# Recurrence output computed transposed, by 32-column matmuls on quarters of the array

## The chip, the cores and the metric

The kernel runs on one core of one Trainium2 chip. The metric is the device time of one launch in microseconds, as the median of several runs. A profile is one execution recorded by the hardware: its span is the time from its first to its last recorded instruction, and its own time holds a little more around it. The engines are TensorE (PE; its weight loads PEld), VectorE (DVE), ScalarE (ACT), GpSimd (POOL) and SyncE (SP), whose queue issues the DMAs.

## What is computed

A gated linear recurrence over 768 steps for 4 batches of 8 heads of 48 channels, and then a feed-forward layer over the 3072 tokens (d_model 384, d_ff 2048). Inputs and output are fp32.

```
def _attn_ref(q, k, v, alpha):
    for t in range(S):
        state = alpha[:, :, t, :, None] * state + np.einsum('bhd,bhe->bhde', k[:, :, t], v[:, :, t])
        y[:, :, t] = np.einsum('bhd,bhde->bhe', q[:, :, t], state)

def _moe_ref(x, w_in, w_out):
    r = np.maximum(x @ w_in, 0.0)
    return (r * r) @ w_out
```

Here x is y with the heads of a token side by side: 8 heads of 48 make the 384 columns. The matmuls of the kernel are in bf16 with fp32 sums.

## The kernel before

**Tiling.** The 3072 tokens are 24 chunks of 128, six for each batch. Within a chunk the recurrence is written as matmuls. L is the log of alpha; a matmul with a triangle of ones (`e_p0`) sums it along the chunk; A and Ainv are its exponentials; qA = q·A and kI = k·Ainv. qA and kI are transposed on TensorE, for two heads at a time (four pairs of heads, `NP`; a head takes 48 of 64 rows), and copied to SBUF as qkT. The scores sc = kI·qA (`e_p2`, by halves of the array, one head in each) are masked into sm. The state of 48x48 a head goes through the PSUM tile st: `e_ps` adds kI·v, VectorE scales it (`e_stm`), ScalarE casts it to sb (`e_sb`).

**The output of a chunk before.** Its output y lies with tokens on partitions: `e_p3a` (L576) multiplies qkT by the last chunk's sb, four matmuls of 96 columns (left out in the first chunk of a batch), and `e_p3b` (L582) multiplies the masked scores by vb, eight matmuls of 48 columns, both with 128x128 weights and into one PSUM bank, py. The feed-forward part needs x transposed, with the 384 channels on partitions. So `add_tail` (L380) follows: ScalarE casts py to bf16 (xn, L374 with `cast`), TensorE transposes xn in three 128x128 blocks into another bank (`e_p4`, recorded at L257), and VectorE, or ScalarE in the first six chunks, copies these to their 128 columns of xT_big (`e_xT`).

**Three ways to work chunks.** The first four chunks are worked as two supers of two chunks each (`add_super`, L597), where a row holds two neighbouring tokens and 64 rows are one chunk; their score part has 64-row weights. Chunks 4 to 7 are worked singly (`add_chunk`, L401). From chunk 8 on (`PAIRS`) the scores of two chunks are taken in one block (`add_scores`, L508), and `add_back` (L545) follows for each.

**The feed-forward part.** The chunks are grouped 4, 1, 1, 2, 2, and so on (`GN`). For each group, `add_moe1` multiplies w_in by xT_big (16 slices of d_ff, three matmuls each), ScalarE takes the relu, VectorE squares into gT; `add_moe2` multiplies gT by w_out in four quarters for each chunk; ScalarE or VectorE copies the sums out and SP issues the store. The weights arrive in fp32 by DMA, in pieces, and are cast by GpSimd or ScalarE (`load_w`).

**Order.** A planner (`Plan`) writes the order of every engine at build time. Each step is an `Op` with an engine (or several, with a duration for each, of which the one that ends first is taken), a planned duration, its dependencies and a priority. A PE step is ready at the end of what it depends on, plus a slack if that is on another engine: `PE_SLACK` of 0.05 us, and 0.25 us once TensorE's plan is past `PE_CALM` (L36, 25 us). `LEAD` (L330, 3.5) says how many chunks the recurrence may run ahead of the feed-forward part. At run time every engine works its list strictly in that order. The planned durations only make the order.

**PSUM.** Two banks hold sc and st for good; the five others are dealt out by the planner: `GLA_BANKS`, two of them, serve the recurrence of single and double chunks (sums, transposes, second scores, py, px), `SUP_BANKS`, four, that of the supers, and three the feed-forward part. A bank is free again when the step named in `gives` is done. While the planner still sees gaps ahead of the first `add_moe2`, it fills them with matmuls on a zero tile (warm).

Of the kernel before, what the change touches and what calls it, by code (L numbers as in the profile page):

```python
# [8 lines left out]
FP32 = mybir.dt.float32  # L9
# [23 lines left out]

LAT = {"PE": 0.13, "ACT": 0.14, "DVE": 0.13, "POOL": 0.25}
PE_SLACK = 0.05
PE_CALM = 25.0  # L36
PAUSES = [(13.0, 1.0), (18.0, 1.0)]


# [107 lines left out]
def kernel(  # L147
# [97 lines left out]
    nc.gpsimd.memset(kI_s[:, :, :, D:], 0.0)  # L245
    ae_s = big.tile([P, NBUF, 2, NP], FP32)
    nc.vector.memset(ae_s, 0.0)
    xT_big = big.tile([P, KT, n_tok], BF16)

    def pin(ins):  # L250
# [2 lines left out]
    def mm(*a, **kw):  # L253
        pin(nc.tensor.matmul(*a, **kw))  # L254

    def tr(*a):
        pin(nc.tensor.transpose(*a))  # L257
# [11 lines left out]
    def psum(op, shape, dt):  # L269
        i = op.slot.bank  # L270
        return banks[i].tile(shape, dt, name=f"bank{i}")
# [6 lines left out]
    def add(eng, dur, emit, *deps, **kw):  # L278
        return plan.add(Op(eng, dur, emit, deps, **kw))
# [47 lines left out]
    SRC = dict(srcs)  # L327
    EARLY = 2 * 3
    PAIRS = 8
    LEAD = 3.5  # L330

    NS = 2
    SIDE = 0
# [38 lines left out]
    def cast(op, out_t, in_t):  # L372
        if op.eng == "ACT":
            pin(nc.scalar.copy(out_t, in_t))  # L374
        elif op.eng == "DVE":
            pin(nc.vector.tensor_copy(out_t, in_t))  # L376
        else:
            pin(nc.gpsimd.tensor_copy(out_t, in_t))

    def add_tail(s, done, first, g):  # L380
        d = C[s]

        def e_xn():
            d["xn"] = work.tile([P, HD], BF16, name="xn")
            cast(xn, d["xn"], d["py"][:, 0:HD])
        xn = add("ACT", 0.36, e_xn, done, **g)
        first.gives = xn

        def e_p4():
            d["px"] = psum(p4, [P, KT, P], BF16)  # L390
            for j in range(KT):
                tr(d["px"][:, j, :], d["xn"][:, j * P:(j + 1) * P], ident_bf)
        p4 = plan.add(Op("PE", 0.165, e_p4, [xn], takes=GLA_BANKS, lat=0.14, **g))

        def e_xT():
            cast(xT, xT_big[:, :, s * P:(s + 1) * P], d["px"])
        xT = add({"ACT": 0.36, "DVE": 0.27} if s < EARLY else "DVE", 0.27, e_xT, p4, prio=-9.0)
        d["x"] = d["end"] = xT
        p4.gives = xT

    def add_chunk(s):  # L401
        d = C[s]
# [11 lines left out]
        def e_vb():  # L414
            d["vb"] = work.tile([P, H, D], BF16, name="vb", bufs=4)
            pin(nc.gpsimd.tensor_copy(d["vb"], d["vt"]))  # L416
        vb = d["use_vt"] = add("POOL", 0.55, e_vb, d["ld_vt"], old, prio=-5.0)

        def e_p0():
            pm = d["pm"] = psum(p0, [P, 512], FP32)  # L420
# [75 lines left out]
            cp = cpk = add("DVE", 0.61, lambda: e_cp(0, 2 * NP), p1k, **g)  # L496
        p1q.gives = cpk

        d.update(cps=[cp, cpk], mk=mk, vb_op=vb, ae1=ae1, kI=kI, ae=ae)
        if s < PAIRS:  # L500
            add_scores(s, 1)
            add_back(s)
        elif s % 2:
            add_scores(s - 1, 2)
            add_back(s - 1)
            add_back(s)

    def add_scores(s, n):  # L508
        pr = C[s:s + n]
# [32 lines left out]
        for hh, h in enumerate(hold):  # L542
            h.gives = pr[1]["sms"][hh]

    def add_back(s):  # L545
        d = C[s]
        b, c = divmod(s, NCH)
        g = dict(prio=-10.0 + s * 0.01)
        last = c == NCH - 1
        kI, ae, mk, vb, ae1 = d["kI"], d["ae"], d["mk"], d["vb_op"], d["ae1"]  # L550
        cp, (sm0, sm1) = d["cps"][0], d["sms"]

        if not last:
            def e_ps():
                if c == 0:
                    state["ps"] = ps_st.tile([P, NP, 2 * D], FP32, name="st")
                st = d["st"] = state["ps"]
                for p in range(NP):
                    mm(st[:, p, :], lhsT=kI[:, 2 * p:2 * p + 2, :], rhs=d["vb"][:, 2 * p:2 * p + 2, :],
                       start=(c == 0 and p == 0), stop=True, skip_group_check=True)  # L560
            prev = C[s - 1].get("sb") if s else None
            if c == 0 and s:
                prev = C[s - 2]["sb"]
            ps = plan.add(Op("PE", 0.17, e_ps, [mk, vb, ae1, prev], lat=0.16, **g))

            def e_stm():
                st4 = d["st"].rearrange("p n (j e) -> p n j e", j=2)
                pin(nc.vector.tensor_mul(st4, st4, bcast(ae, D)))  # L568
            stm = add("DVE", 0.47, e_stm, ps, ae1, prio=-2.0)

            def e_sb():
                d["sbt"] = work.tile([P, NP, 2 * D], BF16, name="sb")
                pin(nc.scalar.copy(d["sbt"], d["st"]))  # L573
            d["sb"] = add("ACT", 0.37, e_sb, stm, prio=-2.0)

        def e_p3a():  # L576
            d["py"] = psum(p3a, [P, 512], FP32)
            for p in range(NP):
                mm(d["py"][:, 2 * p * D:2 * (p + 1) * D], lhsT=d["qkT"][:, p, :], rhs=C[s - 1]["sbt"][:, p, :],
                   start=(p == 0), stop=False, skip_group_check=True)  # L580

        def e_p3b():  # L582
            if c == 0:
                d["py"] = psum(p3b, [P, 512], FP32)
            for hh in range(2):
                for p in range(NP):
                    h = 2 * p + hh
                    mm(d["py"][:, h * D:(h + 1) * D], lhsT=d["sm"][:, hh, p, :], rhs=d["vb"][:, h, :],
                       start=(c == 0 and hh == 0 and p == 0), stop=True, skip_group_check=True)
        p3a = None  # L590
        if c > 0:
            p3a = plan.add(Op("PE", 0.17, e_p3a, [cp, C[s - 1]["sb"], after(sm0)], takes=GLA_BANKS, **g))
        p3b = plan.add(Op("PE", 0.21, e_p3b, [after(sm1, 0.02), sm0, vb, after(p3a)], takes=None if c else GLA_BANKS, lat=0.15, **g))

        add_tail(s, p3b, p3a or p3b, g)

    def add_super(u):  # L597

# [20 lines left out]
            pin(nc.gpsimd.tensor_copy(d["vb"][t], d["vt"][:, :, t, :]))  # L619
        vb = [add("POOL", 0.55, lambda t=t: e_vb(t), d["ld_vt"], *old, prio=-5.0) for t in any_]  # L620
        d["use_vt"] = vb[1]

        d["pm"] = [None, None]
        HC = HD // 2
# [125 lines left out]
        for ab in any_:  # L750
            s = 2 * u + ab
            c = pair[ab]
            r = slice(HF * ab, HF * ab + HF)
            before = C[s - 1].get("sb") if s else None
            if s < NCH - 1:
                def e_ps(c=c, r=r, s=s):
                    if s == 0:
                        state["ps"] = ps_st.tile([P, NP, 2 * D], FP32, name="st")
                    st = c["st"] = state["ps"]
                    for t in any_:  # L760
                        for p in range(NP):
# [12 lines left out]
                c["sb"] = add("ACT", 0.37, e_sb, stm, prio=-12.0)  # L774

            def e_p3a(c=c, r=r, s=s, ab=ab):
                c["py"] = psum(c["p3a"], [P, 512], FP32)
                for p in range(NP):
                    mm(c["py"][:, 2 * p * D:2 * (p + 1) * D], lhsT=qT(p)[:, ab].rearrange("k t c -> k (t c)"), rhs=C[s - 1]["sbt"][:, p, :],
                       start=(p == 0), stop=False, skip_group_check=True)  # L780

            def e_p3b(c=c, r=r, s=s):
                if s == 0:
                    c["py"] = psum(c["p3b"], [P, 512], FP32)
                for x in any_:
                    for hh in range(2):
                        for p in range(NP):
                            h = 2 * p + hh
                            mm(c["py"][:, h * D:(h + 1) * D], lhsT=d["sm"][p // NH][r, hh, x, p % NH, :], rhs=d["vb"][x][r, h, :],
                               start=(s == 0 and x == 0 and hh == 0 and p == 0), stop=(x == 1), skip_group_check=True)  # L790
            p3a = None
            if s:
                p3a = c["p3a"] = plan.add(Op("PE", 0.2, e_p3a, [cq, before], takes=SUP_BANKS, **g))
            p3b = c["p3b"] = plan.add(Op("PE", 0.5, e_p3b, [*sm, *vb, after(p3a)], takes=None if s else SUP_BANKS,
                                         lat=0.15, **g))
            add_tail(s, p3b, p3a or p3b, g)

    GN = [4, 1, 1, 2, 2, 2, 2, 2, 2, 2, 2, 2]
    assert sum(GN) == NT
# [223 lines left out]
```

## Time and profile before

| | |
|---|---|
| runs of the kernel before, us | 186.7, 185.51, 186.2 (median 186.2) |
| profiled execution, its own time | 185.78 us |
| its span | 184.1 us |
| mean granted TensorE clock | 1.00 |
| TensorE matmuls | 1992 |
| DMA bytes, mean rate | 30.23 MB, 164 GB/s |

The largest groups of TensorE are the two feed-forward matmuls, 73.3 us (xT_big with w_in) and 70.9 us (gT with w_out). A profile row names the source line, engine and operation, then out<-in, the shapes as partitions x elements, a count, and behind the bar the busy time, the mean ns of one, and the idle time of the engine before them with what ended it. A matmul's row gives rows*columns of its weights first and then the shape of what is moved. Matmuls are pipelined: the mean of one is from its start to its modelled end, much longer than the step from one start to the next. All matmuls are recorded at one of two helper lines, L254 (`mm`) and L257 (`tr`), so they are told apart by tiles and shapes. A stretch row gives start:end, its length, busy us with counts in brackets for PE, PEld, DVE, ACT and POOL, the granted clock, the DMA engines' busy share and GB/s. A timeline row gives a start, a length, and what ran, with neighbours of one kind merged.

### The profile page before, as it was taken

The numbers are of one execution on the slowest core, as the hardware profiler recorded it, in microseconds if no ns is written. First come the engines' busy times: TensorE is split into PE (matmuls) and PEld (weight loads), VectorE is DVE, ScalarE is ACT, GpSimd is POOL, SyncE is SP. The second block draws the span as 40 slices with busy tenths as digits, with TensorE's granted clock in tenths as the row PEclk, the third lists the DMA queues.
The fourth block names the chain that finished last, engine by engine and source line by source line (L and its number), as shares of the span: only waits on it lengthen the run. The fifth ranks groups of instructions, "written<-read, shape, count | busy, mean of one in ns | idle before, by whom it ended". The sixth has DMA issues, their size and how long they took to land.

```text
span 184.1 us, 5041 instructions
## 1 busy us (share of the span) xinstructions
PE 178.6 (97%) x1992; PEld 133.4 (72%) x1993; DVE 134.8 (73%) x282; ACT 121.9 (66%) x259; POOL 27.6 (15%) x46
## 2 busy tenths in 40 slices
PE   7899999999999999999999999999999999999993
PEld 3567674666987788767867877777877878767763
DVE  6699669447998888856894997966996988852600
ACT  3565879267998598825939857847848768633721
POOL 6024476612011111111011011010010000000000
PEclk9999999999999999999999999999999999999999
DMA  5999999799898989893989899876701101012012
GB/s 139 276 281 323 318 341 375 156 222 212 168 215 174 220 158 214 180 217 84 205 197 209 202 206 201 192 148 149 187 0 43 46 2 48 0 45 89 0 43 85
DMA packets 101352, 30.23 MB, mean 164 GB/s; under 512 B 93776, under 2 KB 100560, under 8 KB 101328
## 3 DMA queue, kind: packets, MB, share of 16 engines
q1 hardware_dynamic: 101328, 29.91, 69.3%
q8 instruction: 15, 0.25, 0.5%
q14 instruction: 9, 0.07, 0.1%
HBM read 25.17 MB, written 4.72 MB: 162 GB/s over the span
## 4 chain that ended last, share of the span: by engine, by line
PE 90%; DVE 4%; DMA 2%; issue 1%; ACT 1%; DVEq 0%
PE bank L254 77%; PE bank L257 8%; DMA qt<-in_q_dram 2%; PE st L254 2%; PE sc L254 2%; DVE qkT L376 1%; DVE sm L726 1%; DVE sm L534 0%; DVE xT_big L376 0%; ACT r L840 0%; DVE qA_s L663 0%; DVE kI_s L663 0%; DVE qA_s L467 0%; ACT A L647 0%; DVE kI_s L473 0%
## 5 line engine op out<-in xcount | busy, mean ns | idle before, releaser
L254 PE MATMUL bank<-xT_big,w_in_b 128*128 128x256 bf16 (+2 forms) x599 | 73.3, 268 | 0.2
L254 PE MATMUL bank<-w_out_b,gT 128*128 128x384 bf16 (+2 forms) x400 | 70.9, 319 | 0.0
L840 ACT ACTIVATE r<-bank 128x512 bf16<-128x512 f32 x96 | 56.1, 602 | 16.1 <-PE bank L254 14.3
L254 PEld LDWEIGHTS <-w_in_b 128*128 128x128 bf16 x600 | 52.8, 98 | 9.3 <-issue 0.3
L848 DVE TENSOR_TENSOR gT<-r 128x512 bf16<-128x512 bf16 x96 | 42.8, 470 | 10.4 <-ACT r L840 10.1
L254 PEld LDWEIGHTS <-gT 128*128 128x128 bf16 x400 | 36.5, 98 | 18.4
L416 POOL CAST vb<-vt 128x384 bf16<-128x384 f32 x20 | 10.8, 542 | 92.0 <-PE bank L254 49.8
L376 DVE COPY qkT<-bank 128x1024 bf16<-128x1024 bf16 (+1 forms) x26 | 16.5, 646 | 4.8 <-PE bank L257 4.6
L912 ACT COPY ob<-bank 128x384 f32<-128x384 f32 x18 | 8.7, 483 | 16.1 <-PE bank L254 15.8
L534 DVE TENSOR_TENSOR sm<-sc,utri_b 128x512 bf16<-128x512 f32 x24 | 15.4, 683 | 3.0 <-PE sc L254 3.0
L374 ACT CAST xn<-bank 128x384 bf16<-128x384 f32 x24 | 11.2, 486 | 9.2 <-PE bank L254 9.1
L254 PEld LDWEIGHTS <-qkT 64*128 64x128 bf16 (+2 forms) x304 | 10.5, 97 | 5.6 <-issue 2.5
L376 DVE COPY xT_big<-bank 128x384 bf16<-128x384 bf16 x19 | 6.7, 354 | 10.5 <-PE bank L257 10.5
L470 DVE TENSOR_TENSOR qA_s<-qt,Af 128x384 bf16<-128x384 f32 x12 | 10.4, 869 | 2.5 <-ACT Af L439 2.5
L411 ACT ACTIVATE L_s<-at 128x384 bf16<-128x384 f32 x20 | 10.2, 523 | 2.1 <-DMA at<-in_alpha_dram 2.0
L439 ACT ACTIVATE Af<-bank 128x384 f32<-128x384 f32 x12 | 10.4, 865 | 1.6 <-ACT xn L374 1.0
L473 DVE TENSOR_TENSOR kI_s<-kt,Ainv 128x384 bf16<-128x384 f32 x20 | 11.3, 566 | 0.0
L443 ACT ACTIVATE Ainv<-bank 128x384 bf16<-128x384 f32 x20 | 10.3, 513 | 0.0
L534 DVE TENSOR_TENSOR sm<-bank,utri_b 128x512 bf16<-128x512 f32 x16 | 10.2, 681 | 0.0
L257 PE MATMUL bank<-ident_bf,qA_s 128*128 128x128 bf16 x96 | 9.5, 223 | 0.6 <-DVE qA_s L663 0.4
L254 PE MATMUL bank<-vb,sm 128*128 128x48 bf16 (+1 forms) x224 | 9.7, 183 | 0.0
L573 ACT CAST sb<-st 128x384 bf16<-128x384 f32 x16 | 7.7, 482 | 2.8 <-DVE st L568 2.6
(70 smaller groups left out, 174.2 us busy)
## 6 DMA issues: line engine op xcount, KB each, us to landing
at<-in_alpha_dram SPq DMA_DIRECT2D x24, 192.0 KB, 3.9
qt<-in_q_dram SPq DMA_DIRECT2D x24, 192.0 KB, 3.8
kt<-in_k_dram SPq DMA_DIRECT2D x24, 192.0 KB, 3.9
vt<-in_v_dram SPq DMA_DIRECT2D x20, 192.0 KB, 3.7
out_dram<-ob SPq DMA_DIRECT2D x19, 192.0 KB, 2.8
wo<-in_moe_w_out_dram SPq DMA_DIRECT2D x4, 768.0 KB, 7.7
wi<-in_moe_w_in_dram SPq DMA_DIRECT2D x4, 384.0 KB, 6.9
wi<-in_moe_w_in_dram SPq DMA_DIRECT2D x2, 768.0 KB, 5.8
```

The source lines that it names most:

```text
L254: pin(nc.tensor.matmul(*a, **kw))
L257: pin(nc.tensor.transpose(*a))
L374: pin(nc.scalar.copy(out_t, in_t))
L376: pin(nc.vector.tensor_copy(out_t, in_t))
L416: pin(nc.gpsimd.tensor_copy(d["vb"], d["vt"]))
L439: pin(nc.scalar.activation(d["A"], split(d["pm"][:, 0:HD], s), AF.Exp))
L443: pin(nc.scalar.activation(d["Ai"], d["pm"][:, 0:HD].rearrange("p (h d) -> p h d", h=H), AF.Exp, scale=-1.0))
L470: pin(nc.vector.tensor_mul(qA[:, :, 0:D].rearrange(v4, j=2), d["qt"].rearrange(v4, j=2), d["A"]))
L473: pin(nc.vector.tensor_mul(kI[:, :, 0:D], d["kt"], d["Ai"]))
L534: pin(nc.vector.tensor_mul(d["sm"][:, hh], d["sc"][hh], utri_b.to_broadcast([P, NP, P])))
L840: pin(nc.scalar.activation(box["r"][:, 0:w], box["ph"][:, 0:w], AF.Relu))
L848: pin(nc.vector.tensor_mul(gT[g][:, f0:f0 + per, lo * P:lo * P + n], r, r))
```

## The change

y of a chunk is computed with channels on partitions and tokens along the free axis: the weights are 32 columns of sb or vb, and what is moved is qkT or sm, 128 tokens wide. The 384 channels are four pairs of heads of 96, each three slices of 32. Slice number 3p + i (pair p, i = 0, 1, 2) goes to quarter q = (3p+i) mod 4 of the array's columns, which is also the quarter of PSUM's partitions, and to block j = (3p+i) div 4: this is the layout that xT_big has. `y_groups` orders the matmuls in turn over the quarters. The state part takes one matmul a slice, 12 in all. In the score part each head has its own scores: slice 0 lies in the first head, slice 2 in the second, and slice 1 has 16 channels of each, so it takes two matmuls, with weights from a new tile vz_s that holds the 16 channels of one head beside zeros: 16 matmuls in all. `e_vz` fills it on GpSimd from vb for each chunk; it is zeroed once at the start.

The cast xn, the transposes and their bank are gone; xT is cast straight from py (fp32 in PSUM), by ScalarE or VectorE as the planner finds. For a double chunk (from number 8 on), one TensorE step holds the y of both chunks and waits for the masks and states of both; a step without an engine holds the first chunk's bank. For the supers, the score part comes in two steps, one for two pairs of heads (`e_yb`, weights of 64 rows and 32 columns), and the state part (`e_ya`) follows. In the planner, `PE_CALM` goes from 25 to 60 us and `LEAD` from 3.5 to 4.0.

```diff
-PE_CALM = 25.0
+PE_CALM = 60.0
+    vz_s = big.tile([P, NBUF, NP, 64], BF16)
+    nc.gpsimd.memset(vz_s, 0.0)
-    LEAD = 3.5
+    LEAD = 4.0
...
-    def add_tail(s, done, first, g):
...
+    def e_vz(vb, i):
+        mid = vb.rearrange("p (n j) d -> p n (j d)", j=2)[:, :, 32:64]
+        pin(nc.gpsimd.tensor_copy(vz_s[:, i].rearrange("p n (a b) -> p n a b", b=16)[:, :, 0::3],
+                                  mid.rearrange("p n (a b) -> p n a b", b=16)))
+
+    def y_groups(pairs, inter):
+        todo = [[] for _ in range(4)]
+        for p in pairs:
+            for i in range(3):
+                j, q = divmod(3 * p + i, 4)
+                for hh in (0,) if inter else ((0,), (0, 1), (1,))[i]:
+                    todo[q].append((q, j, p, i, hh))
+        return [t[n] for n in range(max(map(len, todo))) for t in todo if n < len(t)]
+
+    def v_cols(vb, vz, p, i, hh):
+        if i == 1:
+            return vz[:, p, 32 * hh:32 * hh + 32]
+        return vb[:, 2 * p + hh, 16 * hh:16 * hh + 32]
+
+    def add_xT(s, d, y):
         def e_xT():
-            cast(xT, xT_big[:, :, s * P:(s + 1) * P], d["px"])
-        xT = add({"ACT": 0.36, "DVE": 0.27} if s < EARLY else "DVE", 0.27, e_xT, p4, prio=-9.0)
+            cast(d["end"], xT_big[:, :, s * P:(s + 1) * P], d["py"])
+        d["x"] = d["end"] = add({"ACT": 0.38, "DVE": 0.47}, 0, e_xT, y, prio=-9.0)
...
+        vz = add("POOL", 0.3, lambda: e_vz(d["vb"], i), vb, old, prio=-5.0)
...
+    def add_y(chunks):
+        def e_py(s, op):
+            C[s]["py"] = psum(op, [P, KT, P], FP32)
+        def e_y():
+            e_py(chunks[-1], y)
+            for s in chunks:
+                d, first = C[s], s % NCH > 0
+                for q, j, p, i, _ in y_groups(range(NP), True) if first else ():
+                    mm(d["py"][32 * q:32 * q + 32, j, :], lhsT=C[s - 1]["sbt"][:, p, 32 * i:32 * i + 32],
+                       rhs=d["qkT"][:, p, :], start=(j == 0), stop=False, skip_group_check=True)
+                seen = set()
+                for q, j, p, i, hh in y_groups(range(NP), False):
+                    mm(d["py"][32 * q:32 * q + 32, j, :], lhsT=v_cols(d["vb"], d["vz"], p, i, hh), rhs=d["sm"][:, hh, p, :],
+                       start=(not first and q not in seen), stop=True, skip_group_check=True)
+                    seen.add(q)
+        deps = []
+        for s in chunks:
+            d = C[s]
+            deps += [*d["sms"], d["vz_op"], d["cps"][0]] + ([C[s - 1]["sb"]] if s % NCH else [])
...
+        y = plan.add(Op("PE", dur, e_y, [*deps, *hold], takes=GLA_BANKS, lat=0.15, **g))
+        for s, op in zip(chunks, [*hold, y]):
+            op.gives = add_xT(s, C[s], y)
...
+        def e_yb(v):
+            for x in any_:
+                for q, j, p, w, hh in y_groups(range(NH * v, NH * v + NH), False):
+                    for ab in any_:
+                        r = slice(HF * ab, HF * ab + HF)
+                        mm(pair[ab]["py"][32 * q:32 * q + 32, j, :], lhsT=v_cols(d["vb"][x], vz_s[:, i + x], p, w, hh)[r],
+                           rhs=d["sm"][v][r, hh, x, p - NH * v, :], start=(v == 0 and (ab, q) not in seen),
+                           stop=(x == 1), skip_group_check=True)
...
+                def e_ya(s=s, ab=ab):
+                    for q, j, p, w, _ in y_groups(range(NP), True):
+                        mm(pair[ab]["py"][32 * q:32 * q + 32, j, :], lhsT=C[s - 1]["sbt"][:, p, 32 * w:32 * w + 32],
+                           rhs=qT(p)[:, ab].rearrange("k t c -> k (t c)"), start=False, stop=True, skip_group_check=True)
+                y = plan.add(Op("PE", 0.3, e_ya, [cq, C[s - 1]["sb"], after(y)], lat=0.15, **g))
+            slot.gives = add_xT(s, pair[ab], y)
```

`add_back` becomes `add_state`, which keeps `e_ps`, `e_stm` and `e_sb` as they were; `e_p3a`, `e_p3b` and `add_tail` are gone.

More of the change, by code (lines that the diff above doesn't have):

```diff
@@ L378, in cast @@
             pin(nc.gpsimd.tensor_copy(out_t, in_t))
-    def add_tail(s, done, first, g):
[L381 to L393, printed above, removed]
+    def e_vz(vb, i):
[15 more added lines that the diff above has]
+    def add_xT(s, d, y):
         def e_xT():
-            cast(xT, xT_big[:, :, s * P:(s + 1) * P], d["px"])
-        xT = add({"ACT": 0.36, "DVE": 0.27} if s < EARLY else "DVE", 0.27, e_xT, p4, prio=-9.0)
-        d["x"] = d["end"] = xT
-        p4.gives = xT
+            cast(d["end"], xT_big[:, :, s * P:(s + 1) * P], d["py"])
+        d["x"] = d["end"] = add({"ACT": 0.38, "DVE": 0.47}, 0, e_xT, y, prio=-9.0)
+        return d["end"]
     def add_chunk(s):
@@ L497, in add_chunk @@
         p1q.gives = cpk
-        d.update(cps=[cp, cpk], mk=mk, vb_op=vb, ae1=ae1, kI=kI, ae=ae)
+        d.update(cps=[cp, cpk], mk=mk, vb_op=vb, vz_op=vz, vz=vz_s[:, i], ae1=ae1, kI=kI, ae=ae)
         if s < PAIRS:
             add_scores(s, 1)
-            add_back(s)
+            add_state(s)
+            add_y([s])
         elif s % 2:
             add_scores(s - 1, 2)
-            add_back(s - 1)
-            add_back(s)
+            add_state(s - 1)
+            add_state(s)
+            add_y([s - 1, s])
     def add_scores(s, n):
@@ L543, in add_scores, with add_state @@
             h.gives = pr[1]["sms"][hh]
-    def add_back(s):
+    def add_state(s):
         d = C[s]
@@ L550, in add_back @@
         kI, ae, mk, vb, ae1 = d["kI"], d["ae"], d["mk"], d["vb_op"], d["ae1"]
-        cp, (sm0, sm1) = d["cps"][0], d["sms"]
         if not last:
@@ L574, in add_back @@
             d["sb"] = add("ACT", 0.37, e_sb, stm, prio=-2.0)
[L576 to L595, printed above, removed]
+    def add_y(chunks):
+        g = dict(prio=-10.0 + chunks[-1] * 0.01)
+        hold = []
+        def e_py(s, op):
[16 more added lines that the diff above has]
+            deps += [*d["sms"], d["vz_op"], d["cps"][0]] + ([C[s - 1]["sb"]] if s % NCH else [])
+        for s in chunks[:-1]:
+            h = Op("NIL", 0.0, None, [C[chunks[-1]]["sms"][0], *hold], takes=GLA_BANKS, lat=0.0, **g)
+            h.emit = lambda s=s, h=h: e_py(s, h)
+            hold.append(plan.add(h))
+        dur = sum(0.41 if s % NCH else 0.24 for s in chunks) + 0.19
+        y = plan.add(Op("PE", dur, e_y, [*deps, *hold], takes=GLA_BANKS, lat=0.15, **g))
+        for s, op in zip(chunks, [*hold, y]):
+            op.gives = add_xT(s, C[s], y)
@@ L621, in add_super @@
         d["use_vt"] = vb[1]
+        vz = [add("POOL", 0.3, lambda t=t: e_vz(d["vb"][t], i + t), vb[t], *old, prio=-4.0) for t in any_]
         d["pm"] = [None, None]
@@ L774, in add_super @@
                 c["sb"] = add("ACT", 0.37, e_sb, stm, prio=-12.0)
[L776 to L790, printed above, removed]
@@ L791, in add_super, with e_py @@
-            p3a = None
-            if s:
[L793 to L796, printed above, removed]
+        def e_py(ab, op):
+            pair[ab]["py"] = psum(op, [P, KT, P], FP32)
+        def e_yb(v):
+            if v == 0:
+                e_py(1, yb[0])
+            seen = set()
+            for x in any_:
[5 more added lines that the diff above has]
+                           stop=(x == 1), skip_group_check=True)
+                        seen.add((ab, q))
@@ new lines, in add_super @@
+        hold = Op("NIL", 0.0, None, [sm[0]], takes=SUP_BANKS, lat=0.0, **g)
+        hold.emit = lambda: e_py(0, hold)
+        plan.add(hold)
+        yb = [None, None]
+        for v in any_:
+            yb[v] = plan.add(Op("PE", 0.4, lambda v=v: e_yb(v), [*sm[2 * v:2 * v + 2], *vz, hold, after(yb[0])],
+                                takes=None if v else SUP_BANKS, lat=0.15, **g))
+        for ab, slot in zip(any_, (hold, yb[0])):
+            s = 2 * u + ab
+            y = yb[1]
+            if s:
+                def e_ya(s=s, ab=ab):
[4 more added lines that the diff above has]
+            slot.gives = add_xT(s, pair[ab], y)
```

## The prediction

> **What bounds the kernel now.** I read the page's busy shares and the shares of the chain of waits first, then busy time by four stretches that I chose where the work changes: loading and the four chunks worked in twos, the first feed-forward group, the steady part, the end.
>
> ```profile
> PE 178.6 (97%) x1992; PEld 133.4 (72%) x1993; DVE 134.8 (73%) x282; ACT 121.9 (66%) x259; POOL 27.6 (15%) x46
> ...
> PE 90%; DVE 4%; DMA 2%; issue 1%; ACT 1%; DVEq 0%
> ```
> ```profile
> 10.00:24.00 14.00, 13.42 (x232) 9.90 (x231) 11.63 (x22) 10.10 (x23) 5.34 (x7) 1.00 1.08 309
> 24.00:60.00 36.00, 35.69 (x401) 25.32 (x402) 27.67 (x53) 27.45 (x65) 11.41 (x12) 1.00 0.99 231
> 60.00:160.00 100.00, 99.92 (x1104) 78.42 (x1102) 81.45 (x170) 71.53 (x145) 7.52 (x14) 1.00 0.66 143
> ```
> TensorE carries 90% of the chain, and from 24 us on it is idle for 0.3 us in 36 and 0.1 us in 100, at a granted clock of 1.00. Counted by starts (44.22 plus four matmuls of 0.163 is 44.87, the next starts at 45.15) about 1 us is lost between 24 and 60 us. So from 24 us on the change is worth what TensorE issues less; freed ScalarE time is worth nearly nothing. Before 24 us the latency of the recurrence and the weights' DMA (share 1.08) count.
>
> **What one TensorE step costs.** A busy time holds the last matmul's tail; the pace is (block − mean of one) / (count − 1). From the timeline of TensorE:
> ```profile
> 45.31 0.24 PE L254 MATMUL bank<-ones_col,L_s 128*128 128x1 bf16 x4
> 45.48 0.40 PE L254 MATMUL sc<-qkT 64*128 64x128 bf16 x8
> 45.81 1.01 PE L254 MATMUL bank<-xT_big,w_in_b 128*128 128x128 bf16 x15
> 46.66 0.33 PE L254 MATMUL bank<-sb,qkT 128*128 128x96 bf16 x4
> ...
> 47.17 0.37 PE L254 MATMUL bank<-vb,sm 128*128 128x48 bf16 x8
> ...
> 48.27 0.33 PE L257 MATMUL bank<-ident_bf,xn 128*128 128x128 bf16 x3
> ```
> ```profile
> 16.01 0.34 PE L257 MATMUL bank<-ident_bf,xn 128*128 128x128 bf16 x3
> 16.29 0.42 PE L254 MATMUL sc<-qkT 64*64 64x128 bf16 x16
> ```
> - Transposes: (0.33 − 0.219) / 2 = 56 ns each. State part (sb,qkT): (0.33 − 0.206) / 3 = 42 ns. Score part (vb,sm): (0.37 − 0.183) / 7, about 25 ns.
> - Parts of the array work side by side: sc on two halves takes (0.40 − 0.219) / 7 = 26 ns a matmul; sc on four quarters (64x64) (0.42 − 0.216) / 15 = 14 ns, four per 56 ns.
> - A visit to another division costs a drain each way. The last sc of the first block starts at 45.48 + 0.40 − 0.216 = 45.66 and the next matmul at 45.81: 0.15 instead of 0.056. The way in, from ones_col, is 0.07 over its pace; from the transpose at 16.13 to 16.29, 0.10. I take 0.21 us for a visit, its slower first round included.
>
> **The change, part by part, for the 20 chunks from number 4 on.** Seventeen have a state part (6, 12 and 18 begin a batch).
> - Removed on TensorE: 60 transposes x 56 = 3.36 us, 68 state matmuls x 42 = 2.86, 160 score matmuls x 25 = 4.00: 10.2 us.
> - Added: 12 state matmuls and 16 score matmuls of 128 columns, in rounds of four, one for each 32-column quarter: 3 and 4 rounds. No row shows four column quarters at once. The nearest is 64x64, four parts, but two by rows and two by columns; I take its 56 ns a round, since all four share one pace there and the moved bytes per round are alike. Bounds: 112 ns, if only two column quarters run together as that row shows, and 224 ns, four times the serial 56; below 56 the stream of 128 columns itself stands (the transposes' pace), so a gain from there is excluded. 17 x 3 + 20 x 4 = 131 rounds x 56 = 7.34 us.
> - Added drains: 4 singles and 8 doubles make 12 visits x 0.21 = 2.52 us (bounds: 0, if every visit adjoined another of its kind; 0.43 each, if the way in waited for the whole 0.22 us tail of the matmul before as well). Together 9.9.
> - Sum: 9.9 − 10.2 = −0.3 us.
>
> The Trainium skill (TensorEngine Tiling (Array Packing), Restrictions and Gotchas) says that column tiling gives up the fast weight load. By the figure of its page TensorE: Matmul & The Clock Gate, LDWEIGHTS, 32 columns would then take an estimated 27 ns, four in a row 107 ns a round, and the sum would be +6.4 instead of −0.3 us. The trace's 64x64 rows, whose loads have 64 columns, show four loads hidden in a round of 56 ns, which speaks against a row of loads one by one.
>
> **Other engines.** From the groups with shapes kept apart:
> ```profile
> L374 ACT CAST xn<-bank 128x384 bf16<-128x384 f32 x24 | 11.2, 486 | 9.2 <-PE bank L254 9.1
> L376 DVE COPY xT_big<-bank 128x384 bf16<-128x384 bf16 x19 | 6.7, 354 | 10.5 <-PE bank L257 10.5
> L910 DVE COPY ob<-bank 128x384 f32<-128x384 f32 x5 | 2.8, 552 | 1.2 <-PE bank L254 1.2
> L416 POOL CAST vb<-vt 128x384 bf16<-128x384 f32 x20 | 10.8, 542 | 92.0 <-PE bank L254 49.8
> ```
> The 24 xn copies (11.2 us) leave ScalarE. The xT copy now reads fp32: 552 ns on VectorE by the ob row instead of 354, or 0.48 on ScalarE. If all 24 go to VectorE it has 24 x 0.552 − 6.7 = +6.5 us, at most 88 of 100 in the steady part: still covered by TensorE, so 0; with that cover gone it would be the 6.5. The 24 new vz copies on GpSimd have 128 elements a partition against 384 in 0.54 us: 0.2 to 0.5 us each, on an engine that is idle 92 us ahead of its vb casts; their reader y comes over 4 us after vb (38.09 and 42.75 for chunk 4). The one behind them in its queue is a weight cast, which waits for its DMA anyway. The memset of vz_s, twice the 512 elements of kI_s (0.53 us), ends near 4.5 us; GpSimd then sits idle until 9.49. No DMA is added; SP's order changes only by the planner.
>
> **The start.** One copy and one TensorE hop leave each chunk's latency.
> ```profile
> 20.70 0.83 POOL L303 CAST w_in_b<-wi 128x768 bf16<-128x768 f32 x1 [0.29 <-DMA wi<-in_moe_w_in_dram]
> ...
> 21.83 0.57 PE L254 MATMUL bank<-vb,sm 64*128 64x48 bf16 x16
> ...
> 22.54 0.48 ACT L374 CAST xn<-bank 128x384 bf16<-128x384 f32 x1
> ...
> 23.69 0.36 DVE L376 COPY xT_big<-bank 128x384 bf16<-128x384 bf16 x1 [1.24 <-PE bank L257]
> ...
> 29.87 1.47 POOL L303 CAST w_out_b<-wo 128x1536 bf16<-128x1536 f32 x1 [1.19 <-DMA wo<-in_moe_w_out_dram]
> ```
> Chunk 3's x lands at 24.05 and the dense stream starts at 24.10. After: its state is cast at 20.23, y can follow, x is there near 21.3. Then the weight cast that ends at 21.53 is late next: one more pair of columns of 0.65 us, and the stream starts at 22.2, 1.9 us earlier. The w_out casts give part back: the fourth ends at 34.19 + 1.47 = 35.66, and its first matmul stood at 36.72, a slack of 1.06, or 0.8 without the 0.27 us step just ahead of it. I take −0.8, between 0 and −1.9. Chunk 4's x (45.20) gets earlier by the xn hop too (43.15 to 44.73, 1.6 us), so that this is not lost there.
>
> **Stalls.** The planner's slack after a foreign engine stays 0.05 instead of 0.25 us up to 60 us, while a copy planned at 0.36 to 0.38 takes 0.48: matmuls are placed ahead of their operands. Shorter chains take from the 1 us of stalls. Bounds −1.0 and +1.5; I take −0.1. LEAD lets the recurrence run half a chunk further ahead; where TensorE always has a matmul to issue this is worth 0.
>
> **Sum.** −0.3 − 0.8 − 0.1 = −1.2 us. The profiled execution is 185.78 (span 184.1 and 1.7 around it), so 184.6; the median of three, 186.2, lies 0.4 above it: 185.0.
>
> **The rivals.**
> - *Column quarters run two at a time* (the slower one). Place: each y block. For it: no row shows four. Against it: the 64x64 rows. Price 131 x 56 = 7.3 us more: 192.3. By the Trainium skill's rule on the weight load, above, it would end near here too, by loads in a row. It decides once a round takes over 80 ns (131 x 24 ns = 3.1 us, that is 188.1).
> - *The short slack bites.* Between 24 and 60 us TensorE, in order, waits at y for masks, vz and sb of two chunks, with feed-forward matmuls queued behind it. +1.5, and the start gains nothing: 185.0 + 1.6 + 0.8 = 187.4. For it: ScalarE and VectorE are 76% and 77% busy there. Against it: TensorE's idle time there is 0.3 us now.
> - *The start keeps its 1.9 us* and 0.7 of the stalls go: 185.0 − 1.1 − 0.6 = 183.3. For it: x of every chunk comes about 1.5 us earlier. Against it: w_out.
> - *It frees only what TensorE hides*: xn gone, no change at the start: 186.2 − 0.3 = 185.9, inside the forecast's own range.
>
> **Chances.** About 1% (1.9 us) is what a measurement of this kernel can tell from no change. Forecast, 184.0 to 186.0, 0.51: 0.10 of it faster by over 1% (under 184.3), 0.41 within. Start kept, 0.20: faster. Short slack, 0.16: half within, half slower. Two at a time, 0.13: slower. So faster 0.30, same 0.49, slower 0.21. The range from 182.8 to 187.9 leaves out the 0.13 and tails.
>
> **What would show it.** In the changed profile: y matmuls of 128x32 at 14 ns a matmul (28 in about 0.4 us), 0.15 us between such a block and its neighbours, no xn, xT copies near 0.5 us, the dense stream from about 23 us, TensorE idle under 1 us between 24 and 160. A round over 80 ns, or waits of TensorE for sb or sm before y that sum to over 1.5 us, would make it wrong.

## The result and the profile after

| | before | after |
|---|---|---|
| median of six runs, us | 186.16 | 190.69 |
| lowest and highest, us | 185.51 and 186.70 | 189.25 and 192.37 |
| profiled execution, its own time (span), us | 185.78 (184.1) | 192.37 (190.7) |

The ratio is 1.0239 [1.0207, 1.0271]: slower by 2.4%, on the other side of what was forecast and outside the range (182.8 to 187.9). Ratios leave out executions more than 1.5% above the fastest of their kernel; the profiled ones of the changed kernel, of E2 and of E11 are among these, so the readings of the changed kernel are held against a second profile of it (run E17), and E2, of whose four runs only one is left, has no ratio.

First the page of the changed kernel, busy shares and the chain of waits by engine.

```profile
PE 179.6 (94%) x2306; PEld 128.6 (67%) x2306; DVE 136.2 (71%) x275; ACT 117.4 (62%) x244; POOL 35.1 (18%) x69
...
PE 61%; DMA 15%; DVE 7%; SPq 6%; ACT 5%; issue 3%; POOL 2%; DVEq 0%; ACTq 0%; POOLq 0%
```

TensorE's busy time is up by only 1.0 us, but it carries 61% of the chain where it carried 90%, and there are two names that were hardly there before: DMA, 15%, and SPq, the queue of SP, 6%. Something waits for transfers, and for their turn to be issued. The busy times by stretch say where (start:end, length, busy us of PE, PEld, DVE, ACT and POOL, granted clock, DMA share, GB/s).

```profile
24.00:60.00 36.00, 35.76 (x453) 24.97 (x452) 28.61 (x53) 25.79 (x61) 12.99 (x17) 1.00 0.96 228
60.00:160.00 100.00, 95.22 (x1209) 71.09 (x1208) 77.24 (x152) 64.27 (x130) 13.31 (x30) 0.98 0.67 144
```

From 24 to 60 us TensorE is as full as before. In the steady part it is idle for 4.78 us of 100, where it was idle for 0.08, and the mean clock is 0.98. TensorE is not slowed by its new matmuls; it stands still. (E17's profile has 95.23 us busy in the same 100.) The groups name the wait.

```profile
L576 DVE TENSOR_TENSOR st<-st,ae_s 128x384 f32<-128x384 f32 x16 | 8.9, 558 | 4.2 <-DMA ae_s<-Af 3.9 <-PE st L256 0.2
L376 ACT CAST xT_big<-bank 128x384 bf16<-128x384 f32 x14 | 6.7, 481 | 5.6 <-PE bank L256 5.5
L378 DVE CAST xT_big<-bank 128x384 bf16<-128x384 f32 x10 | 5.6, 556 | 3.8 <-PE bank L256 3.8
L384 POOL COPY vz_s<-vb 128x128 bf16<-128x128 bf16 x24 | 8.6, 372 | 0.8
```

The last three are as forecast. The first is `e_stm`: VectorE stands for 3.9 us ahead of it, for the DMA ae_s<-Af; in the kernel before, the same step stood for 0.5 us and none of it for a DMA:

```profile
L568 DVE TENSOR_TENSOR st<-st,ae_s 128x384 f32<-128x384 f32 x16 | 8.9, 557 | 0.5 <-PE bank L254 0.3 <-PE st L254 0.2
```

This DMA was not in the prediction's working at all. From chunk 12 on (`TURN`), ae, the total decay of a chunk, is not computed by ScalarE but fetched from the last row of the exponential Af by two tiny DMAs (0.8 KB each), which stand in SP's queue among the loads and stores. The code is in both kernels:

```
        def e_aed():
            for j in range(2):
                pin(nc.sync.dma_start(out=ae_s[HF * j:HF * j + D, i, j], in_=d["Af"][P - 1:P, j]))
```

SP issues its list in the planner's order, one DMA after another. So ae can hold up the loads behind it until Af is there, and loads that are held can hold up ae. Both happen. That ae holds the queue is not new: its issues waited for ScalarE for 25.4 us in all in the kernel before, and for 21.7 us in the changed one. What differs is where the waits fall. The timeline of the changed kernel around the largest wait (start, length, what ran; in brackets the idle time of the engine ahead of it and what ended it):

```profile
111.94 0.86 ACT L446 ACTIVATE Af<-bank 128x384 f32<-128x384 f32 x1 [0.27 <-PE bank L256]
...
114.19 2.56 SPq L350 DMA_DIRECT2D kt<-in_k_dram  x1
...
116.85 0.69 SPq L350 DMA_DIRECT2D vt<-in_v_dram  x1
...
117.59 0.70 SPq L350 DMA_DIRECT2D at<-in_alpha_dram  x1
...
118.38 1.53 SPq L463 DMA_DIRECT2D ae_s<-Af  x2
...
121.47 0.57 DVE L576 TENSOR_TENSOR st<-st,ae_s 128x384 f32<-128x384 f32 x1 [3.50 <-DMA ae_s<-Af]
121.95 0.68 DVE L378 COPY qkT<-bank 128x1024 bf16<-128x1024 bf16 x1
...
122.69 0.61 PE L256 MATMUL bank<-qkT 64*128 64x128 bf16 x8 [2.69 <-DVE qkT L378]
```

Read it from the bottom. TensorE waits 2.69 us for the copy of qkT. That copy is short, and its operand had long been there: it stands behind st in VectorE's queue. st waits 3.50 us for ae. ae needs Af, which ended at 111.94 + 0.86 = 112.80, but the two DMAs are issued at 118.38, 5.6 us later, since SP is busy with loads until then, one of which held the queue for 2.56 us. In the kernel before, the DMAs of the same chunk were issued 1.8 us after their Af:

```profile
111.10 0.86 ACT L439 ACTIVATE Af<-bank 128x384 f32<-128x384 f32 x1
...
113.77 1.28 SPq L456 DMA_DIRECT2D ae_s<-Af  x2
```

The other direction is seen earlier, at chunk 15's load of alpha (at). SP's queue before:

```profile
76.99 0.85 SPq L348 DMA_DIRECT2D at<-in_alpha_dram  x1
...
83.84 2.00 SPq L456 DMA_DIRECT2D ae_s<-Af  x2
```

and after, with what follows on ScalarE and TensorE:

```profile
80.32 1.22 SPq L463 DMA_DIRECT2D ae_s<-Af  x2
...
82.86 1.62 SPq L350 DMA_DIRECT2D at<-in_alpha_dram  x1
...
87.03 0.52 ACT L417 ACTIVATE L_s<-at 128x384 bf16<-128x384 f32 x1 [1.67 <-DMA at<-in_alpha_dram]
...
88.09 0.81 PE L256 MATMUL bank<-xT_big,w_in_b 128*128 128x256 bf16 x6 [1.07 <-ACT r L871]
```

The planner put the first ae ahead of at, no longer behind it. The load is issued 5.9 us later, the log of alpha is late on ScalarE, a relu stands behind that in ScalarE's queue, and TensorE waits 1.07 us for the relu's bank and 0.36 us once more. With 0.65 us at 79.05 (a bank that the second scores hold) these make 4.77 of the 4.78 us. Two of the four cannot be put down to ae: the 0.65 us ended before the first ae was issued, at 80.32, and the 0.36 us is still there in E9 below, where ae is out of SP's queue and the load of alpha goes out at 80.50. That leaves 2.69 + 1.07 = 3.8 us for the queue.

The long wait costs more than its length. The granted clock in stretches of 3 us around it:

```profile
122.00:125.00 3.00, 2.31 (x16) 1.53 (x17) 3.00 (x8) 1.19 (x3) 0.00 (x0) 0.51 0.80 174
125.00:128.00 3.00, 3.00 (x40) 1.68 (x41) 1.82 (x4) 0.61 (x2) 0.00 (x0) 0.92 1.12 221
```

2.31 us of work at 0.51 and 3.00 us at 0.92 lose 2.31 x 0.49 + 3.00 x 0.08 = 1.4 us. The Trainium skill (TensorE: Matmul & The Clock Gate, Why this matters for your kernels) asks for no idle gap of TensorE over some 3 us, else the clock halves; the trace agrees on the halving, but it came after a gap of 2.69 us already. In E8's profile a wait of 2.26 us at 120 us was enough (0.73 and 0.70 in two stretches of 3 us from 120 on), while in E1's one of 1.66 us left the clock at 1.00. The runs fit the size: of the nine executions of the changed kernel behind its ratios (on record and E17), the three with a mean clock of 0.999 or 1.00 took 189.25, 189.71 and 189.96 us, and the six with 0.990 or 0.991 took 190.65 to 192.68, with a median of 191.2: 1.5 us apart.

Of the 6.6 us by which the profiled spans differ, 4.7 are waits of the steady part and some 1.4 the clock; I could not place the other half microsecond.

### The profile page after: what moved, and what is told of

The parts are those of the page before. It is cut to its first block, busy times and chain, and to the rows that moved or that the text cites. A ratio compares the mean times of both kernels' runs of the same rounds, so it can differ in the third digit from the quotient of the medians.

```text
span 190.7 us, 5668 instructions
## 1 busy us (share of the span) xinstructions
PE 179.6 (94%) x2306; PEld 128.6 (67%) x2306; DVE 136.2 (71%) x275; ACT 117.4 (62%) x244; POOL 35.1 (18%) x69
## 4 chain that ended last, share of the span: by engine, by line
PE 61%; DMA 15%; DVE 7%; SPq 6%; ACT 5%; issue 3%; POOL 2%; DVEq 0%; ACTq 0%; POOLq 0%
PE bank L256 54%; DMA wo<-in_moe_w_out_dram 5%; DMA at<-in_alpha_dram 5%; SPq L350 4%; DMA vt<-in_v_dram 4%; PE bank L259 4%; DVE sm L543 2%; PE sc L256 2%; ACT r L871 1%; PE st L256 1%; ACT w_in_b L309 1%; DMA ae_s<-Af 1%; POOL w_out_b L305 1%; ACT Af L446 1%; DVE half_in L222 1%
## 5 line engine op out<-in xcount | busy, mean ns | idle before, releaser
L256 PE MATMUL bank<-w_out_b,gT 128*128 128x384 bf16 (+2 forms) x400 | 70.0, 321 | 0.2 <-POOL w_out_b L305 0.2
L871 ACT ACTIVATE r<-bank 128x512 bf16<-128x512 f32 x96 | 56.9, 600 | 20.1 <-PE bank L256 18.0
L256 PEld LDWEIGHTS <-gT 128*128 128x128 bf16 x400 | 37.5, 98 | 22.4 <-issue 2.0
L943 ACT COPY ob<-bank 128x384 f32<-128x384 f32 x15 | 7.2, 480 | 13.8 <-PE bank L256 11.3
L417 ACT ACTIVATE L_s<-at 128x384 bf16<-128x384 f32 x20 | 10.1, 523 | 5.6 <-DMA at<-in_alpha_dram 5.6
L480 DVE TENSOR_TENSOR kI_s<-kt,Ainv 128x384 bf16<-128x384 f32 x20 | 12.2, 610 | 0.0
L576 DVE TENSOR_TENSOR st<-st,ae_s 128x384 f32<-128x384 f32 x16 | 8.9, 558 | 4.2 <-DMA ae_s<-Af 3.9
L256 PEld LDWEIGHTS <-qkT 64*128 64x128 bf16 (+1 forms) x224 | 5.7, 99 | 6.7 <-DVE qkT L378 4.1
L376 ACT CAST xT_big<-bank 128x384 bf16<-128x384 f32 x14 | 6.7, 481 | 5.6 <-PE bank L256 5.5
L450 ACT ACTIVATE Ainv<-bank 128x384 bf16<-128x384 f32 x20 | 10.1, 506 | 0.0
L256 PE MATMUL bank<-sm,vb 128*32 128x128 bf16 (+1 forms) x224 | 10.0, 220 | 0.0
```

The source lines that it names most:

```text
L417: pin(nc.scalar.activation(L[:, :, 0:D], d["at"], AF.Ln))
L450: pin(nc.scalar.activation(d["Ai"], d["pm"][:, 0:HD].rearrange("p (h d) -> p h d", h=H), AF.Exp, scale=-1.0))
L480: pin(nc.vector.tensor_mul(kI[:, :, 0:D], d["kt"], d["Ai"]))
L871: pin(nc.scalar.activation(box["r"][:, 0:w], box["ph"][:, 0:w], AF.Relu))
```

## The experiments

Four theories were set against each other. A: the planner's two new constants make the waits. B: the single TensorE step for two chunks does. C: the weight casts that moved to ScalarE come late and push everything. D, formed from the traces of the first four runs: the ae DMAs and the loads in SP's one queue. Ratios are to the kernel before, on the same chip.

**E1 to E4: the constants.**

```diff
E1
-PE_CALM = 60.0
+PE_CALM = 25.0
-    LEAD = 4.0
+    LEAD = 3.5
E2
-PE_CALM = 60.0
+PE_CALM = 25.0
E3
-    LEAD = 4.0
+    LEAD = 3.5
E4, in the kernel before
-PE_CALM = 25.0
+PE_CALM = 60.0
-    LEAD = 3.5
+    LEAD = 4.0
```

> The changed kernel with PE_CALM 25 and LEAD 3.5 as before; only the planner's order differs. Theory A (the two constants let the recurrence and its 16-byte ae DMAs be placed ahead of loads that have not landed): about 185.5 us, and the waits of TensorE between 60 and 160 us, 4.8 us in the changed kernel, fall under 1 us. Theory B (a double chunk's y, which waits for both chunks and holds both recurrence banks): stays at 189 to 191 us. Theory C (the start: weights cast on ScalarE, all later loads 2 us late): stays near 189 us unless the start's order happens to change.

> The changed kernel with PE_CALM 25 alone (LEAD 4.0 kept). Theory A with the slack as the cause: about 186 us; with LEAD as the cause: 190 us. Theories B and C: 189 to 191 us.

> The changed kernel with LEAD 3.5 alone (PE_CALM 60 kept). Theory A with LEAD as the cause: about 186 us, with the first ae DMA again behind the loads of chunk 15; with the slack as the cause: 190 us. Theories B and C: 189 to 191 us.

> The kernel before with PE_CALM 60 and LEAD 4.0; its output path is untouched. Theory A: 188 to 190 us. Theories B and C: within 1 us of 186.2.

| | us | ratio | TensorE idle, 60 to 160 us |
|---|---|---|---|
| E1 old constants | 188.69 | 1.0106 [1.003, 1.0181] | 2.59 |
| E2 old PE_CALM | 193.88, lowest 190.18 | none | 5.80 |
| E3 old LEAD | 187.45 | 0.9994 [0.9948, 1.004] | 1.39 |
| E4 before, new constants | 187.32 | 1.0024 [0.9987, 1.0061] | 1.07 |

LEAD 4.0 is what separates the changed kernel from the one before (E3), but by itself it is nearly free (E4). PE_CALM at 25 us is no better than at 60 with the new path (E1 against E3), so the short slack, the prediction's second rival, is not the cause. What LEAD does has to go through something else. In E1 the dense stream is 0.9 us ahead of the kernel before at 66 us; then VectorE's st waits 1.64 us at 102 and 2.09 us at 118 for ae, and TensorE 0.93 and 1.66 us with it. E3's VectorE still waits 3.0 us for ae in all, but TensorE stands only 1.12 us behind it. This suggested that the constants only choose which of these waits meets TensorE, and theory D was formed.

**E5 to E8: another queue for ae, and the weights.** E5 is the changed kernel with the edit shown, E6 the same with LEAD 3.5, E7 the same in the kernel before; E8 lets only GpSimd cast the weights.

```diff
E5, E6, E7
-                pin(nc.sync.dma_start(out=ae_s[HF * j:HF * j + D, i, j], in_=d["Af"][P - 1:P, j]))
+                pin(nc.scalar.dma_start(out=ae_s[HF * j:HF * j + D, i, j], in_=d["Af"][P - 1:P, j]))
E6 as well
-    LEAD = 4.0
+    LEAD = 3.5
E8
-        if n < 4:
-            eng["ACT"] = 0.1 + 0.32 * n
```

> The changed kernel, all constants as changed; the two small ae DMAs of each chunk from 12 on are issued from ScalarE's queue, right behind the exponential that makes their source, and no longer from SP's. Theory D (on SP's one queue the ae DMA, which waits for ScalarE, stands ahead of loads, and loads stand ahead of ae DMAs; VectorE then waits in order for ae and TensorE for VectorE): the waits of TensorE from 60 us on, 4.8 us in the profile of the changed kernel, fall under 1.5 us and the time to 186 to 187.5. Theory B (the double chunk's y and its two banks): no change, 189 to 191. Theory C (the late weights): waits fall little, 188 to 190.

> As e5 with LEAD 3.5. Theory D: the 1.3 us wait at 120 us of e3 goes too: 185 to 186, below the kernel before of the same chip by about 0.5%. Theories B and C: as e3, 187.4.

> The kernel before with the same move of the ae DMAs. Theory D: it has little to win, since TensorE lost only 0.2 us after 80 us there: 186 to 187, within 0.5% of before. If the queue mattered for both alike it would fall to 185.

> The changed kernel with all casts of weights on GpSimd, which takes the four small w_in casts from ScalarE, where one stood behind a relu. Theory C: the last w_out cast ends near 35.7 us again instead of 37.4, the loads behind it come 1.5 us sooner and the time falls to 187 or less. Theory D: the start gains under 1 us, and the waits at 79, 87 and 120 us stay for the most part: 188 to 190.

E5 took 191.56 us, 1.0268 [1.0176, 1.0359]; E6 191.34, 1.0251 [1.0144, 1.0358]; E7 189.76, 1.0168 [1.0111, 1.0225]; E8 190.24, 1.02 [1.0127, 1.0274]. VectorE's wait for ae was gone in E5 (0.9 us ahead of st, all of it for TensorE), and yet it is no faster. E7, the control, shows why; its timeline:

```profile
83.89 1.96 ACTq L456 DMA_DIRECT2D ae_s<-Af  x2
...
85.90 0.94 ACT L411 ACTIVATE L_s<-at 128x384 bf16<-128x384 f32 x2 [1.72 <-issue]
```

The two DMAs take 1.96 us on ScalarE's queue, and ScalarE's next work stands 1.72 us for nothing but this issue. Issuing from ScalarE costs the kernel before 1.7% by itself, which drowns what it removes. The run tells nothing for or against D; it had to be asked with an idle engine. E8 brought the last w_out cast from 37.41 back to 35.33 us and kept the waits for the relu, 1.08 and 0.37 us at 86 and 87 us, and 2.26 us at 120 us: C is at most a small part.

**E9 to E12: an idle engine's queue.** E9 is the changed kernel with ae on GpSimd's queue and nothing else; the planner's order stays as it was.

```diff
E9
-                pin(nc.sync.dma_start(out=ae_s[HF * j:HF * j + D, i, j], in_=d["Af"][P - 1:P, j]))
+                pin(nc.gpsimd.dma_start(out=ae_s[HF * j:HF * j + D, i, j], in_=d["Af"][P - 1:P, j]))
E10
-            add_y([s - 1, s])
+            add_y([s - 1])
+            add_y([s])
E11
-    LEAD = 4.0
+    LEAD = 3.5
-        if n < 4:
-            eng["ACT"] = 0.1 + 0.32 * n
E12: E11 and E9 together
```

> The changed kernel, the ae DMAs issued from GpSimd's queue, so that neither SP nor ScalarE spends anything on them (in e5 each of the 24 issues took about 0.6 us of ScalarE). Theory D: without e5's price the time falls under 188, and VectorE no longer waits for ae. If it stays at 189 to 191, the loads that come late are a cause of their own and D holds only a part.

> The changed kernel with one y step for each chunk also in double chunks (add_y for s-1, then for s); constants as changed. Eight more visits to the divided array cost 1.6 us of TensorE. Theory B (one step that waits for both chunks and holds both recurrence banks): the waits after 60 us fall under 1.5 us, the time to 187 or 188 in spite of the visits. Theories A and D: the waits stay, 190 to 192.

> LEAD 3.5, all weight casts on GpSimd. Theory C as a smaller cause beside LEAD: the 1.0 us wait for w_out at 32 us of e3 goes, and the time is 0.5 to 1 us under e3's ratio: 0.994 to 0.997 of before.

> LEAD 3.5, weight casts and the ae DMAs on GpSimd. Theory D: the wait of 1.3 us at 120 us of e3 goes as well: 0.985 to 0.992 of before, the 1.2 us that were forecast of the change. If GpSimd is slow to issue a DMA, vb behind it is late and nothing is won.

| | us | ratio | TensorE idle, 60 to 160 us |
|---|---|---|---|
| E9 | 186.47 | 0.9983 [0.9947, 1.0019] | 0.40 |
| E10 | 190.4 | 1.022 [1.0171, 1.0269] | 3.07 |
| E11 | 187.3 | 1.0011 [0.997, 1.0053] | 1.78 |
| E12 | 185.09 | 0.993 [0.989, 0.9969] | 0.00 |

E9 decides it. Its two DMAs of chunk 16 and the step that reads them, in the timeline and then st's group:

```profile
109.32 0.86 ACT L446 ACTIVATE Af<-bank 128x384 f32<-128x384 f32 x1 [0.63 <-PE bank L256]
...
110.48 1.00 POOL L463 DMA_DIRECT2D ae_s<-Af  x2 [1.15 <-ACT Af L446]
```
```profile
L576 DVE TENSOR_TENSOR st<-st,ae_s 128x384 f32<-128x384 f32 x16 | 8.9, 555 | 0.5 <-PE st L256 0.5
```

ae is issued 0.3 us after its Af, not 5.6; VectorE's wait for it is gone; TensorE's idle time falls from 4.78 to 0.40 us; and with LEAD at 4.0, the short slack, the paired y and the late casts all in place, the 2.4% are gone. So B falls with E9, which keeps the paired y. E10 says less: with two separate y steps the time stays, but its eight more visits cost an estimated 1.6 us and its waits are 3.07 us instead of 4.78. E11 against E3 leaves nothing for C.

**E13 to E16: the control, and the other combinations.** E13 is the edit of E9 in the kernel before. E14 is E9 with LEAD 3.5, E15 E9 with both old constants, E16 E9 with the weights on GpSimd.

```diff
E13, E14, E15, E16
-nc.sync.dma_start(out=ae_s[ ...
+nc.gpsimd.dma_start(out=ae_s[ ...
E14, E15
-    LEAD = 4.0
+    LEAD = 3.5
E15
-PE_CALM = 60.0
+PE_CALM = 25.0
E16
-        if n < 4:
-            eng["ACT"] = 0.1 + 0.32 * n
```

> The kernel before with the ae DMAs on GpSimd's queue: the control for e9. Theory D as a cost of the change (its order lets ae and loads collide on SP, that of before does not): 0.995 to 1.002 of before, since TensorE has almost no waits after 60 us there. If SP's queue cost both kernels alike: 0.975 to 0.985, and the change itself would be slower by 2% still.

> The changed output path with PE_CALM 60, LEAD 3.5 and the ae DMAs on GpSimd; weight casts as in the changed kernel. With both causes off: 0.985 to 0.993 of before, the 1.2 us forecast of the output path. If 0.998 or more, the path saves nothing even undisturbed.

> As e14 with PE_CALM 25 too, so that only the output path and the ae queue differ from before. Theory D: the waits at 103 and 118 us of e1 (2.9 us) go: 0.985 to 0.997. If PE_CALM matters by itself: near 1.005.

> The changed kernel (LEAD 4.0, PE_CALM 60) with the ae DMAs and all weight casts on GpSimd. Theory C as a smaller cause: e9's wait of 0.4 us for w_out at 32 us goes and loads come 1 us sooner: 0.990 to 0.996. Otherwise as e9, 0.998.

E13 took 186.0 us, 0.9957 [0.9931, 0.9983]; E14 186.03, 0.9959 [0.9922, 0.9995]; E15 186.33, 0.9979 [0.9945, 1.0013]; E16 186.27, 0.9972 [0.9939, 1.0005]. The edit alone gives the kernel before 0.4%, so it is no gain of 2.4% that any kernel would have: it removes what the change brought. And once ae is out of SP's queue the constants and the weights no longer matter: E9, E14, E15 and E16 lie within 0.24% of one another and their intervals overlap. That settles A: as far as these intervals can tell, LEAD hurt only through ae's place in SP's queue. The same four say what the new path is worth by itself: held against E13, the kernel before with the same queue, they gain nothing that shows.

**E17 and E18: the two ends once more.** E17 is the changed kernel, E18 is E12, both without any new edit.

> The changed kernel once more, unedited, beside before on the same chip, for a second look at where it waits. Theory D: waits of TensorE at the same three places of the order as in the first profile (near 79, 87 and 120 us), with the first ae DMA ahead of the loads of chunk 15 on SP's queue; 1.015 to 1.03 of before.

> The kernel of e12 once more: it was the lowest of five that differ little, so part of its 0.993 may be the choice. 0.992 to 0.997; if 0.998 or more, it does not stand out from e9, e14 and e16.

E17 took 191.37 us, 1.0232 [1.015, 1.0313], and its profile has the waits at the same places (2.85, 0.81, 0.38 and 0.73 us). Around the largest:

```profile
117.76 1.59 SPq L463 DMA_DIRECT2D ae_s<-Af  x2
...
121.03 0.56 DVE L576 TENSOR_TENSOR st<-st,ae_s 128x384 f32<-128x384 f32 x1 [3.44 <-DMA ae_s<-Af]
...
122.24 0.61 PE L256 MATMUL bank<-qkT 64*128 64x128 bf16 x8 [2.85 <-DVE qkT L378]
```

E18 took 185.63 us, 0.9933 [0.9898, 0.9967]. So E12's version (the new path, ae and the weights on GpSimd, LEAD 3.5) beats both kernels, twice, by 0.7%. How much of that is the new path is not separable: the kernel before with ae on GpSimd stands at 0.9957, and the intervals overlap.

## Why the prediction was wrong

**Right: the pace and the drains.** The y of two chunks in the steady part, from the timeline of TensorE:

```profile
68.80 0.35 PE L256 MATMUL bank<-qkT,sb 128*32 128x128 bf16 x12
...
69.54 0.22 PE L256 MATMUL bank<-sm,vb 128*32 128x128 bf16 x1
69.69 0.34 PE L256 MATMUL st<-vb,kI_s 128*128 128x96 bf16 x4
```

The 56 matmuls start between 68.80 and 69.54: 0.745 us for 55 steps, 13.6 ns each (13.1 in single chunks), where the forecast took 14. So four column quarters share a round, and the rival "two at a time" falls; E9 ends where that rival could not. The Trainium skill's rule that column tiling gives up the fast weight load (TensorEngine Tiling (Array Packing), Restrictions and Gotchas) cost nothing that shows here: the forecast's estimate for that case was 27 ns a matmul. A visit's drain is 0.09 us in and 0.10 out, 0.19 against 0.21. In the sum, TensorE's own steps from chunk 4 on save 1.5 to 1.8 us and pay 1.1 us of drains ahead of the y blocks, some −0.5 us against −0.3.

**Right: the other engines.** The fp32 casts of xT take 481 and 556 ns (0.48 and 0.552 forecast), the vz copies 372 ns (0.2 to 0.5). VectorE is at 77% in the steady part; what it lacks there is ae, not time.

**Wrong, but without effect: the start.** "I take −0.8, between 0 and −1.9". By the starts of the same feed-forward matmuls the changed kernel is 0.4 us behind at 31 us and 0.8 at 35 to 41, because the planner gave four w_in casts to ScalarE (one before), one of them behind a relu, and the last w_out cast ends at 37.41 instead of 35.66 us; E17's profile of the same kernel is 0.2 us ahead at 31 us and 0.2 behind at 35. E1, E8 and E9 have the gain, −0.2 to −0.7 us at 31 to 35 us. But it is not carried: at 68 us the changed kernel is level with the one before (−0.3), and E12's profile, 1.2 us behind at 35 us, is level at 68 as well. To about 80 us the DMA engines are near full in both kernels; I take it that the loads set the pace there, which was not tried.

**Wrong, and the cause of the miss: the stalls.** Two sentences carried it: that LEAD, "where TensorE always has a matmul to issue", "is worth 0", and "No DMA is added; SP's order changes only by the planner". The second is true, but the new order was priced at nothing. The term for stalls, −0.1 with bounds from −1.0 to +1.5, looked at PE_SLACK and at 24 to 60 us; the runs put +4.8 us of waits and, in most executions, some 1.4 us of clock in its place, all after 60 us; 3.8 us of the waits, and the clock behind the longest, go back to the order of SP's queue. With it the condition of the first sentence was gone: TensorE had no matmul to issue. The working followed the instructions that the change adds and removes on four engines, but never listed what stands in SP's queue, so that the wait of `e_stm` for a DMA issued behind loads was not seen. In the trace of before it lay open: ae was issued 1.8 us behind its Af at 113.77, right after a load of alpha, and VectorE did not have to wait.

**The rivals.** "The short slack bites" (187.4) had the sign, but not the mechanism: the old slack is no faster. "It frees only what TensorE hides" (185.9, that is 0.998 of the kernel before) is near what is left once the side effect is taken away: E9 stands at 0.9983. That the numbers meet is in part luck, since moving ae gives the kernel before 0.4% as well (E13): the gain of 1.2 us that was forecast, 0.6%, appears in none of E9, E14, E15 and E16 against E13, and E12 and E18 are lower by no more than 0.3%.

**Left open.** What exactly decides that the planner's new order meets the loads badly (at 83 and 118 us in the changed kernel, at 102 and 118 us in E1) was seen in the traces, not tried one order against another. The clock's share is worked out from rows and from two sets of executions, not from a run that removes it alone; none of the three at full clock was profiled, and their waits may have been shorter. What makes the waits of 0.65 us at 79.05 and 0.36 us at 89.27 is not known. And E9 takes two things off SP at once, the waits in order and the time of 24 issues of some 0.58 us; that the order is the larger part is read from the rows (5.6 us late, against 1.53 us for its own issue), not tried.

## What to carry to other kernels

Before a change that lets a planner rewrite the order, list what each in-order queue holds, the DMA queue included, and ask of every DMA that waits for an engine what stands behind it, and of every DMA that an engine waits for what stands ahead of it. A tiny transfer between engines does not belong in the queue of the bulk loads: on the queue of an idle engine it cost nothing here, on a busy engine's queue 1.7%. And when a tuned constant hurts only together with a change (1.0024 alone, 1.0239 with it), look for the resource through which the two meet before taking the constant back.

## What the hardware showed that was not expected

- A DMA issued by ScalarE held ScalarE: in E7 two took 1.96 us of its queue at 83.89 (1.17 us at 88.26), and 1.72 us of idle time behind the first are booked to the issue alone. On GpSimd two took 1.00 us, on SP 1.2 to 2.0 us.
- The Trainium skill (DMA: Bandwidth & Descriptors, Issuing engines are not separate DMA queues) says that issuing from several engines only saves the time of the sequencer that issues. In this case more hung on it: E9 moved two tiny DMAs a chunk and took the ratio from 1.0239 to 0.9983, and the ae of chunk 16, whose own issue took 1.53 us, had stood behind other issues for 5.6 us.
- One wait of 2.69 us, in a stream that is otherwise full, was followed by half of TensorE's clock for some 3 us (0.51, then 0.92 in stretches of 3 us); the same came behind 2.85 us (E17: 0.62, then 0.81) and 2.26 us (E8: 0.73, then 0.70). In all three the two stretches together lack 0.57 x 3 = 1.7 us of clock, as much as 3.4 us at half speed: a wait of another length cost the same.
- Quarters of 128 rows by 32 columns step every 13.1 to 13.6 ns with 128 columns moved, and the eighths that the supers use (64 rows by 32 columns) every 9.7 to 10.1 ns.
